# Maxima of q: rounded parts computed first and sent by a second DMA queue, unrounded maxima kept in PSUM

## The chip, the cores and the metric

One NeuronCore of a Trainium2 chip runs the whole program: TensorE (PE) multiplies matrices into PSUM, VectorE (DVE), ScalarE (ACT) and GpSimd (POOL) do the rest, and SyncE (SP) issues DMAs; ScalarE has a DMA queue too. The metric is the device time of one execution in microseconds (us), as the median of three runs.

## What is computed

Attention with a feature map, then two MLPs. For each of 4 batches and 8 heads, with 576 positions and 64 features a head:

```python
proj = x @ w_phi                                    # 64 -> 128, for q and for k
proj = proj - max(abs(proj), axis=-1)               # one maximum per position
phi  = concat(exp(proj), exp(-proj))
num  = phi_q @ (phi_k.T @ v);  den = phi_q @ sum(phi_k) + 1e-6
x    = num / den                                    # 2304 x 512 over all heads
x    = ((x @ w1) * (x @ w2)) @ w3 @ w_out           # first MLP, 1024 wide
h    = max(x @ w_in, 0);  out = (h * h) @ w_out2    # second MLP, 2048 wide
```

All inputs are fp32. Products that need the precision are made of three passes over a rounded "high" part and a "low" part, the rest that rounding leaves.

## The kernel before

Heads go two at a time: a *pair* is two heads of one batch, so there are 16 pairs, numbered 0 to 15 here. The attention part runs one *slot* a pair. The order inside a slot is written out by hand: `START` (line 29) is the prologue, `SLOT` (line 35) a list of step names; `step` (line 677) looks each name up and calls it for the pair that it is due for, and every engine then executes its own instructions in the order in which the steps issued them. In slot t, project_q, project_k, the peaks, exp and values work on pair t, the turning of q and k (turn_k, high_k, low_k, turn_q, high_q, low_q) on pair t+1, and the output, keep and the denominators on pair t-1. Even pairs also project the tail positions of k for two pairs (project_k2, peak_k2, less_k2, exp_k2); odd pairs instead turn tails for the next two (turn_tails, keep_tails, low_tail). Between these steps run decode steps of the MLP weights.

The maxima of q take this way. `project_q` (lines 369 to 382) leaves the projection in PSUM, three banks that one pair at a time can use. `max_q` (VectorE, line 387) reduces it to a 128 x 36 tile of maxima. `max_rows` (TensorE, line 395) transposes that. `max_parts` (lines 397 to 408) folds four groups of columns into the final 36 x 32 maxima `m`, makes a rounded copy `mh[:, 0]` by a second reduction, subtracts for the low part `mh[:, 1]`, and two DMAs write the two parts as rows 0 and 1 of `mrow` (SBUF to SBUF, 4.5 KB each). `minus_q` (line 414) multiplies `mrow` by a matrix of -1 and adds the result onto the projection in PSUM. `exp_q` (line 421) reads that twice for the two exponentials. The next pair's project_q writes the same PSUM banks, so it stands behind both.

The part of `SLOT` that matters: `peak_k0 max_rows high_k less_k0 max_parts w-1 late store_x exp_k0 out ... keep`. On ScalarE this is high_k, exp_k0 (two exponentials), keep (a copy), exp_k1, high_q, in odd slots keep_tails, and exp_q twice. On VectorE it is less_k0, the three instructions of max_parts, peak_k1, less_k1, low_k, denominators, low_q, decode work, and reciprocals, whose transpose is the last before the next max_q.

The PSUM banks with tag "o" (two of them) serve pm, po and pd in turn.

Of the kernel before, what the change touches and what calls it, by code (L numbers as in the profile page):

```python
# [9 lines left out]
F32 = mybir.dt.float32  # L10
# [3 lines left out]
ALU = mybir.AluOpType  # L14
AX = mybir.AxisListType
PSUM = bass.MemoryType.PSUM

P = 128
# [26 lines left out]
def attention_then_mlps(ctx: ExitStack, tc: tile.TileContext, q, k, v, w_phi, w1, w2, w3, wo, wi2, wo2, out):  # L45
    nc = tc.nc
# [28 lines left out]
    ident = const.tile([P, P], F32, name="ident")  # L75
# [128 lines left out]
    with ExitStack() as actx:  # L204
        att = actx.enter_context(tc.tile_pool(name="att", bufs=2, side="right"))
        ps = actx.enter_context(tc.tile_pool(name="ps", bufs=3, space=PSUM))

        def bank(name, tag="t", bufs=3):
            return ps.tile([P, 512], F32, tag=tag, bufs=bufs, name=name)
# [48 lines left out]
        nb = S // 32  # L258
# [132 lines left out]

        def max_rows(z):

            z["pm"] = bank(f"pm_{z['nm']}", "o", 2)[:, 0:P]
            nc.tensor.transpose(z["pm"], z["m1"], ident)

        def max_parts(z):
            pm = z["pm"][0:2 * nb]
            m = att.tile([2 * nb, 32], F32, tag="m", name=f"m_{z['nm']}")
            nc.vector.tensor_reduce(m, pm.rearrange("p (a r) -> p r a", a=4), AX.X, ALU.max)  # L400
            mh = att.tile([2 * nb, 2, 32], F32R, tag="mh", name=f"mh_{z['nm']}")
            nc.vector.tensor_reduce(mh[:, 0], pm.rearrange("p (a r) -> p r a", a=4), AX.X, ALU.max)
            nc.vector.tensor_tensor(out=mh[:, 1], in0=m, in1=mh[:, 0].bitcast(F32), op=ALU.subtract)
            z["mrow"] = mrow
            for s in range(2):
                nc.sync.dma_start(
                    z["mrow"][s:s + 1].bitcast(F32).rearrange("s (k r) -> s k r", r=32), mh[:, s].bitcast(F32)
                )

# [136 lines left out]
        w2h, w3s_at, queue, loaded, halves = {}, {}, [], [], []  # L546
# [55 lines left out]
        def even(f, *at):  # L602
# [3 lines left out]
        steps = {  # L606
            "keep_values": (-1, keep_values),
            "project_q": (0, project_q), "max_q": (0, max_q), "max_rows": (0, max_rows), "max_parts": (0, max_parts),
            "minus_q": (0, minus_q), "exp_q0": (0, lambda z: exp_q(z, 0)), "exp_q1": (0, lambda z: exp_q(z, 1)),
            "turn_k": (1, turn_k), "high_k": (1, high_k), "low_k": (1, low_k),  # L610
# [82 lines left out]
        with tc.manual_schedule(engines=mine):  # L693
            for entry in START:
                name, t = entry.split("/")
# [16 lines left out]
    def lunit(dtype, shape, name, tag="w", bufs=RIGHT):  # L712
        return late.tile([P] + shape, dtype, tag=tag, bufs=bufs, name=name)
# [207 lines left out]
    with tc.manual_schedule(engines=mine):  # L921
# [95 lines left out]
        for at, (b, n) in enumerate(mlp2):  # L1017
            cs, nt = nxt, n // P
            ops = None
            for j in range(NR):  # L1020
# [25 lines left out]
                r = lunit(F32R, [2, 512], f"r_{b}_{j}", "g", 3)  # L1046
# [50 lines left out]
```

## Time and profile before

| what | value |
|---|---|
| median of 3 runs | 939.31 us (939.11 to 940.91) |
| the profiled execution | 940.55 us, of which its span 938.8 us |
| TensorE busy | 919.8 us, 98% of the span |
| TensorE weight loads busy | 758.8 us, 81% |
| VectorE busy | 545.3 us, 58% |
| ScalarE busy | 382.6 us, 41% |
| GpSimd busy | 249.2 us, 27% |
| attention part | 0 to about 192 us |

The shares of busy time are means over very different stages: attention takes the first fifth, the rest is nearly all matrix multiplication. A wait is read from the time lines and from the view of waits, where "A <- B" says that A was released by B. A row of several instructions is one group: its start, the stretch that it covers, and how many there are.

### The profile page before, as it was taken

How to read it: one execution, taken by the hardware profiler on the slowest of the kernel's cores; microseconds unless marked ns; L12 is line 12 of the kernel's file. 1: busy time of each engine (PE TensorE's matmuls, PEld its weight loads, DVE VectorE, ACT ScalarE, POOL GpSimd, SP SyncE). 2: the span in 40 equal slices, each digit the busy share in tenths (PEclk: the TensorE clock that was granted, in tenths of full speed). 3: DMA queues.
4: the chain of work that ended last, by engine and by line, in shares of the span. 5: the costliest groups of instructions: out<-in, count | busy, mean ns of one | idle time of the engine just before them, and what ended most of it. 6: DMA issues, size and time to landing. Idle time of an engine off the chain costs nothing.

```text
span 938.8 us, 14821 instructions
## 1 busy us (share of the span) xinstructions
PE 919.8 (98%) x5897; PEld 758.8 (81%) x5897; DVE 545.3 (58%) x892; ACT 382.6 (41%) x689; POOL 249.2 (27%) x304
## 2 busy tenths in 40 slices
PE   8999999999999999999999999999999999999997
PEld 6777777778888988888988888888888888888896
DVE  6888888878656456666856688852224223322332
ACT  4777777643422433432333344342223223222322
POOL 2655566453121123333423145520000000000000
PEclk9999999999999999999999999999999999999999
DMA  6455556245242334254542433211002000200100
GB/s 178 124 154 152 139 157 198 78 144 172 73 135 66 114 114 156 68 202 157 173 176 93 142 118 107 90 46 44 1 1 90 1 0 1 68 1 1 39 8 22
DMA packets 81109, 89.22 MB, mean 95 GB/s; under 512 B 44624, under 2 KB 65680, under 8 KB 81040
## 3 DMA queue, kind: packets, MB, share of 16 engines
q1 hardware_dynamic: 79712, 87.72, 29.5%
q8 instruction: 46, 0.75, 0.3%
q10 hardware_dynamic: 1328, 0.56, 0.3%
q14 instruction: 23, 0.19, 0.1%
HBM read 69.76 MB, written 18.35 MB: 94 GB/s over the span
## 4 chain that ended last, share of the span: by engine, by line
PE 88%; DVE 6%; ACT 3%; DMA 2%; issue 1%; SPq 0%; ACTq 0%
PE ph L183 21%; PE op L905 21%; PE yp L887 11%; PE pb L183 11%; PE pa L183 10%; PE pf L844 5%; PE po L459 2%; PE pkv L432 2%; DMA mrow<-mh 2%; PE pk L250 1%; PE pq L380 1%; DVE kmax L348 1%; ACT qp L421 1%; DVE m L387 1%; PE pd L481 1%
## 5 line engine op out<-in xcount | busy, mean ns | idle before, releaser
L905 PE MATMUL op<-w_w,r 128*128 128x512 f32 x864 | 209.6, 390 | 0.1
L905 PEld LDWEIGHTS op<-w_w,r 128*128 128x128 f32 x864 | 161.1, 188 | 33.4 <-ACT r L1047 0.5
L183 PE MATMUL ph<-y,w_w 128*128 128x512 f32 (+1 forms) x768 | 163.9, 362 | 0.0
L1041 DVE SCALAR_TENSOR_TENSOR r<-ph,t 128x512 f32<-128x512 f32 (+1 forms) x80 | 51.1, 638 | 187.8 <-ACT t L1039 187.8
L183 PEld LDWEIGHTS ph<-y,w_w 128*128 128x128 f32 x768 | 133.3, 189 | 23.8
L1039 ACT ACTIVATE t<-ph 128x512 f32<-128x512 f32 (+1 forms) x80 | 44.5, 556 | 215.4 <-PE ph L183 215.4
L887 PE MATMUL yp<-g,w3o 128*128 128x512 f32 (+1 forms) x480 | 106.1, 370 | 0.0
L129 POOL TENSOR_TENSOR dt_w<-dt_w,dy_w 128x512 f32<-128x512 f32 x48 | 62.9, 1310 | 126.5 <-DVE dy_w L124 126.4
L887 PEld LDWEIGHTS yp<-g,w3o 128*128 128x128 f32 x480 | 83.7, 189 | 14.9 <-DVE yp L873 0.2
L183 PE MATMUL pa<-c,w_w12a 128*128 128x512 f32 (+1 forms) x432 | 93.6, 366 | 0.0
L183 PE MATMUL pb<-c,w_w12b 128*128 128x512 f32 (+1 forms) x432 | 93.6, 366 | 0.0
L183 PEld LDWEIGHTS pa<-c,w_w12a 128*128 128x128 f32 x432 | 75.1, 189 | 13.2
L183 PEld LDWEIGHTS pb<-c,w_w12b 128*128 128x128 f32 x432 | 75.2, 189 | 13.1
L1049 DVE TENSOR_TENSOR r<-r,r 128x512 fp32r<-128x512 f32 (+1 forms) x80 | 51.0, 638 | 41.2 <-ACT r L1047 37.5
L966 DVE TENSOR_TENSOR g<-pb,a 128x512 f32<-128x512 f32 (+1 forms) x39 | 24.8, 636 | 83.9 <-PE pb L183 79.4
L139 POOL TENSOR_TENSOR w_w<-dt_w,w_w 128x512 fp32r<-128x512 f32 x32 | 48.5, 1518 | 84.2 <-ACT w_w L137 84.2
L1047 ACT ACTIVATE r<-r 128x512 fp32r<-128x512 f32 (+1 forms) x80 | 47.2, 590 | 55.9 <-DVE r L1041 55.9
L506 POOL TENSOR_SCALAR rc<-dc 32x9 f32<-32x9 f32 x128 | 45.4, 355 | 57.6 <-DVE dc L496 50.5
L968 ACT ACTIVATE g<-g 128x512 fp32r<-128x512 f32 (+1 forms) x39 | 23.0, 589 | 91.6 <-DVE g L966 91.6
L958 ACT COPY a<-pa 128x512 f32<-128x512 f32 (+1 forms) x39 | 21.2, 543 | 81.0 <-PE pa L183 81.0
L365 ACT ACTIVATE kp<-kp 128x512 f32<-128x512 f32 (+1 forms) x80 | 46.9, 588 | 17.6 <-DVE kp L358 15.5
L121 DVE TENSOR_SCALAR dy_w<-dt_w 128x512 int32<-128x512 int32 x48 | 49.8, 1038 | 0.7
(135 smaller groups left out, 1277.6 us busy)
## 6 DMA issues: line engine op xcount, KB each, us to landing
x<-x_hbm SPq DMA_DIRECT2D x16, 512.0 KB
raw_w<-in_moe_w_dram SPq DMA_DIRECT2D x16, 512.0 KB
raw_w<-in_moe_w_in_dram SPq DMA_DIRECT2D x16, 512.0 KB
raw_w<-in_moe_w_out_dram SPq DMA_DIRECT2D x16, 512.0 KB
qm<-in_q_dram SPq DMA_DIRECT2D x32, 128.0 KB
km<-in_k_dram SPq DMA_DIRECT2D x16, 256.0 KB
vs<-in_v_dram SPq DMA_DIRECT2D x32, 128.0 KB
raw_wo<-in_moe_w_out_dram SPq DMA_DIRECT2D x8, 512.0 KB
```

Of the source, the lines that this page charges most:

```text
L121: nc.vector.tensor_scalar(out=e, in0=t, scalar1=-(1 << 23), scalar2=None, op0=ALU.bitwise_and)
L129: nc.gpsimd.tensor_tensor(out=w, in0=t.bitcast(F32), in1=e.bitcast(F32), op=ALU.add)
L139: nc.gpsimd.tensor_tensor(out=dst[:, 1], in0=w[0], in1=dst[:, 0].bitcast(F32), op=ALU.subtract)
L183: nc.tensor.matmul(ps[:, 0:n], a, c, start=kk + i == 0, stop=kk == KD - 1 and i == 2)
L365: nc.scalar.activation(z["kp", j][:, :, s, :], z["kp", j][:, :, 1, :], AF.Exp, scale=1.0 - 2.0 * s)
L506: nc.gpsimd.tensor_scalar(out=z["rc2"][i * 32:(i + 1) * 32, s, :], in0=z["dc"][at * 32:(at + 1) * 32, :], scalar1=1e-6, scalar2=None, op0= ...
L844: nc.tensor.matmul(pf, a, c, start=g + j + n == 0, stop=g == 1 and j == 3 and n == 2)
L887: nc.tensor.matmul(blk.yp[i][:, 0:blk.n], a, d, start=c % HG + s == 0, stop=c % HG == HG - 1 and s == 2)
L905: nc.tensor.matmul(ops[i], a, d, start=j + s == 0, stop=j == NR - 1 and s == 2)
L1041: nc.vector.scalar_tensor_tensor(out=r32[:, 0:n], in0=ph[:, 0:n], scalar=0.0, in1=t[:, 0:n], op0=ALU.max, op1=ALU.mult)
L1047: nc.scalar.activation(r[:, 0, 0:n], r32[:, 0:n], AF.Copy)
L1049: nc.vector.tensor_tensor(out=r[:, 1, 0:n], in0=r32[:, 0:n], in1=r[:, 0, 0:n].bitcast(F32), op=ALU.subtract)
```

## The change

`max_parts` makes the rounded maxima with its first reduction and the unrounded ones with its second. The unrounded ones no longer have an SBUF tile: they go to columns 128 to 159 of the PSUM bank that holds the transposed maxima, so `z["pm"]` is now the whole bank. The high part's DMA is issued by ScalarE, the low part's by SyncE. `START` and `SLOT` stay as they are.

```diff
         def max_rows(z):
 
-            z["pm"] = bank(f"pm_{z['nm']}", "o", 2)[:, 0:P]
-            nc.tensor.transpose(z["pm"], z["m1"], ident)
+            z["pm"] = bank(f"pm_{z['nm']}", "o", 2)
+            nc.tensor.transpose(z["pm"][:, 0:P], z["m1"], ident)
 
         def max_parts(z):
-            pm = z["pm"][0:2 * nb]
-            m = att.tile([2 * nb, 32], F32, tag="m", name=f"m_{z['nm']}")
-            nc.vector.tensor_reduce(m, pm.rearrange("p (a r) -> p r a", a=4), AX.X, ALU.max)
+            view = z["pm"][0:2 * nb, 0:P].rearrange("p (a r) -> p r a", a=4)
             mh = att.tile([2 * nb, 2, 32], F32R, tag="mh", name=f"mh_{z['nm']}")
-            nc.vector.tensor_reduce(mh[:, 0], pm.rearrange("p (a r) -> p r a", a=4), AX.X, ALU.max)
+            nc.vector.tensor_reduce(mh[:, 0], view, AX.X, ALU.max)
+            m = z["pm"][0:2 * nb, P:P + 32]
+            nc.vector.tensor_reduce(m, view, AX.X, ALU.max)
             nc.vector.tensor_tensor(out=mh[:, 1], in0=m, in1=mh[:, 0].bitcast(F32), op=ALU.subtract)
             z["mrow"] = mrow
-            for s in range(2):
-                nc.sync.dma_start(
+            for s, queue in enumerate((nc.scalar, nc.sync)):
+                queue.dma_start(
                     z["mrow"][s:s + 1].bitcast(F32).rearrange("s (k r) -> s k r", r=32), mh[:, s].bitcast(F32)
                 )
```

On ScalarE, in the slot of pair 9 (kT and qT are the turned k and q, kp the exponents of k, nd the kept numerators, tT the tails, qp the exponentials of q), before:

```order
L291 ACTIVATE kT_2_1819<-pkt_2_1810 128x512
L365 ACTIVATE kp_1_0_1821<-kp_1_0_1821 128x4x128 x2
L488 COPY nd_0_1861<-po_0_1835 128x512
L365 ACTIVATE kp_1_1_1859<-kp_1_1_1859 128x4x128 x2
L291 ACTIVATE qT_2_1885<-pqt_2_1863 128x512
L291 ACTIVATE tT_2_1890<-ptt_2_1869 128x256
L421 ACTIVATE qp_1_1892<-pq_1_1776 128x1152 x2
```

and the same place now:

```order
L291 ACTIVATE kT_2_1810<-pkt_2_1801 128x512
L406 DMA mrow<-mh_1_1814 1x36x32
L365 ACTIVATE kp_1_0_1812<-kp_1_0_1812 128x4x128 x2
L488 COPY nd_0_1851<-po_0_1825 128x512
L365 ACTIVATE kp_1_1_1849<-kp_1_1_1849 128x4x128 x2
L291 ACTIVATE qT_2_1875<-pqt_2_1853 128x512
L291 ACTIVATE tT_2_1880<-ptt_2_1859 128x256
L421 ACTIVATE qp_1_1882<-pq_1_1767 128x1152 x2
```

The DMA of the high part now stands between high_k and exp_k0 of every slot; nothing else moved on ScalarE.

On VectorE, in the same slot (pm is the transposed maxima, kmax the peaks of k), before:

```order
L358 TENSOR_TENSOR kp_1_0_1821<-pk_1_0_1790,kmax_1_0_1815 128x4x128
L400 TENSOR_REDUCE m_1_1823<-pm_1_1817 36x32
L402 TENSOR_REDUCE mh_1_1825<-pm_1_1817 36x32
L403 TENSOR_TENSOR mh_1_1825<-m_1_1823,mh_1_1825 36x32
L348 TENSOR_REDUCE kmax_1_1_1857<-pk_1_1_1798 128x4
```

and now:

```order
L358 TENSOR_TENSOR kp_1_0_1812<-pk_1_0_1781,kmax_1_0_1806 128x4x128
L400 TENSOR_REDUCE mh_1_1814<-pm_1_1808 36x32
L402 TENSOR_REDUCE pm_1_1808<-pm_1_1808 36x32
L403 TENSOR_TENSOR mh_1_1814<-pm_1_1808,mh_1_1814 36x32
L348 TENSOR_REDUCE kmax_1_1_1847<-pk_1_1_1789 128x4
```

The two reductions changed places, and the unrounded result is written to PSUM and read from there; the count and the neighbours are the same.

On SyncE, around the same slot's maxima (qm, km and vs are loads of q, k and v, raw_w12a of a weight), before:

```order
L236 DMA qm_3_1771<-in_q_dram 128x4x64 x2
L227 DMA km_3_1774<-in_k_dram 128x2x256
L406 DMA mrow<-mh_1_1825 1x36x32 x2
L105 DMA raw_w12a_1830<-in_moe_w_dram 128x4x128
L533 DMA x_hbm_1_81<-xm_1_1582 128x1024
```

and now:

```order
L236 DMA qm_3_1762<-in_q_dram 128x4x64 x2
L227 DMA km_3_1765<-in_k_dram 128x2x256
L406 DMA mrow<-mh_1_1814 1x36x32
L105 DMA raw_w12a_1820<-in_moe_w_dram 128x4x128
L533 DMA x_hbm_1_81<-xm_1_1574 128x1024
```

One of the two DMAs to mrow left SyncE; the loads before and behind it stand as they stood.

## Rows read from the trace of the kernel before

**Rows 1.** Windows: stretch, length, busy us of PE, PEld, DVE, ACT, POOL; clock, DMA, GB/s

```profile
60.00:120.00 60.00, 56.99 (x817) 44.44 (x815) 52.49 (x99) 47.64 (x85) 35.97 (x66) 1.00 0.53 143
...
400.00:600.00 200.00, 200.00 (x951) 168.37 (x950) 140.38 (x204) 74.19 (x133) 73.15 (x53) 1.00 0.41 141
```

**Rows 2.** Waits, 0 to 340 us: who <- for whom: us in total, times, longest

```profile
PE pq L414 <- DMA mrow<-mh: 6.4, 7, 1.2
...
ACT qp L421 <- PE pq L414: 2.2, 3, 1.0
```

**Rows 3.** DMA issues of two lines: count, ns min/median/max, first and last start

```profile
L406 SPq DMA_DIRECT2D mrow<-mh x32: 733/786/908, 13.1 to 183.5; - x32
...
L242 ACTq DMA_DIRECT2D ktl<-in_k_dram x2: 615/626/637, 2.7 to 3.7; - x2
```

**Rows 4.** Time line, start: start us, us, engine, line, what, count [idle before <-releaser]

```profile
2.74 1.59 ACTq L242 DMA_DIRECT2D ktl<-in_k_dram  x2
...
3.02 1.31 SPq L236 DMA_DIRECT2D qm<-in_q_dram  x2
...
4.36 1.28 ACT L148 ACT_TABLE_LOAD   x1 [4.36 <-DMA qm<-in_q_dram]
```

**Rows 5.** Time line of the slot of pair 9, with its end

```profile
114.75 0.27 DVE L400 TENSOR_REDUCE m<-pm 36x32 f32<-36x128 f32 x1
114.87 1.29 ACT L365 ACTIVATE kp<-kp 128x512 f32<-128x512 f32 x2
...
116.19 0.59 ACT L488 COPY nd<-po 128x512 f32<-128x512 f32 x1
...
116.80 1.30 ACT L365 ACTIVATE kp<-kp 128x512 f32<-128x512 f32 x2
...
118.14 0.60 ACT L291 ACTIVATE qT<-pqt 128x512 fp32r<-128x512 f32 x1
...
118.63 0.38 ACT L291 ACTIVATE tT<-ptt 128x256 fp32r<-128x256 f32 x1
118.77 0.69 DVE L294 TENSOR_TENSOR qT<-pqt,qT 128x512 fp32r<-128x512 f32 x1 [0.70 <-ACT qT L291]
...
119.01 2.15 ACT L421 ACTIVATE qp<-pq 128x1152 f32<-128x1152 f32 x2
...
121.36 0.96 PE L380 MATMUL pq<-qT,wss 64*128 64x512 f32 x6
...
122.96 1.34 DVE L387 TRANSPOSE_TENSOR_REDUCE m<-pq 128x36 f32<-128x1152 f32 x1
```

**Rows 6.** Time line of the slot of pair 8, with its end

```profile
103.39 1.29 ACT L365 ACTIVATE kp<-kp 128x512 f32<-128x512 f32 x2 [0.32 <-DVE kp L358]
...
105.32 1.29 ACT L365 ACTIVATE kp<-kp 128x512 f32<-128x512 f32 x2 [0.17 <-DVE kp L358]
...
106.52 0.58 ACT L291 ACTIVATE qT<-pqt 128x512 fp32r<-128x512 f32 x1
...
107.69 0.87 ACT L365 ACTIVATE kp<-kp 128x256 f32<-128x256 f32 x2 [0.58 <-DVE kp L358]
107.71 0.76 PE L414 MATMUL pq<-mrow,minus 128*128 128x512 f32 x3 [0.98 <-DMA mrow<-mh]
...
108.50 2.15 ACT L421 ACTIVATE qp<-pq 128x1152 f32<-128x1152 f32 x2
...
110.86 0.97 PE L380 MATMUL pq<-qT,wss 64*128 64x512 f32 x6
...
112.15 1.38 DVE L387 TRANSPOSE_TENSOR_REDUCE m<-pq 128x36 f32<-128x1152 f32 x1 [0.66 <-PE pq L380]
```

**Rows 7.** Time line: end of pair 0's slot, loads in pair 10's, pair 15's split of x

```profile
19.33 0.97 PE L380 MATMUL pq<-qT,wss 64*128 64x512 f32 x6 [0.71 <-ACT qp L421]
...
125.71 1.27 SPq L242 DMA_DIRECT2D ktl<-in_k_dram  x2
...
184.08 1.90 DVE L149 TENSOR_TENSOR x<-x,x 128x512 fp32r<-128x512 f32 x3 [1.27 <-ACT x L148]
```

## The prediction

> **What bounds the kernel now.** I read the busy time by stretch first. In the attention part (0 to 190 us) no engine is full: between 60 and 120 us TensorE is busy 56.99 of 60 us, VectorE 52.49, ScalarE 47.64, and they hand work to each other; later (400 to 600 us) TensorE alone is full, 200.00 of 200.00 [rows 1]. The change touches attention only, so it is worth what it does to the length of the sixteen slots there; a microsecond lost there is a microsecond lost at the end.
>
> Then the waits. TensorE waits 6.4 us in 7 places for the transfer that writes the rows of maxima, and ScalarE three times, 2.2 us, for the matmuls behind it [rows 2]. That is what the change could take away. Last I read two slots in order of time, pair 9 (odd) and pair 8 (even), to see which engine sets their ends.
>
> Odd pair 9 [rows 5]: on ScalarE exp_k0 starts at 114.87; keep, exp_k1, high_q, keep_tails and exp_q follow at 116.19, 116.80, 118.14, 118.63 and 119.01 almost without a gap, and exp_q ends at 119.01 + 2.15 = 121.16. The next project_q starts at 121.36. VectorE's low_q waited 0.70 us for ScalarE's high_q (118.77), and max_q of the next pair (122.96) shows no idle time before it: VectorE ran from low_q into it. So in an odd slot ScalarE's row of activations sets both the next project_q and, through low_q, the next max_q.
>
> Even pair 8 [rows 6]: ScalarE waits 0.17 before exp_k1 and 0.58 before exp_k2, TensorE waits 0.98 for the transfer (107.71), exp_q ends at 108.50 + 2.15 = 110.65 and the next project_q starts at 110.86. Here ScalarE has room.
>
> **The change, part by part.**
>
> *High part on ScalarE's queue.* In the order given above, the transfer stands between high_k and exp_k0 on ScalarE and waits for VectorE's first reduction. Queued behind the wait are exp_k0, keep, exp_k1, high_q and both exp_q: everything the slot needs from ScalarE. The reduction starts at 114.75 [rows 5]; I give it the 0.27 us of its kind, which is how far the trace's two reductions of this shape go, and 0.03 us of hand-over, so the transfer can be issued at 115.05. Its issue takes 0.786 us on SyncE (733 to 908 ns); ScalarE's own issues of loads take 0.626 us [rows 3]. Does the issue hold ScalarE's next instruction? The trace has one place: ScalarE's last two load issues run from 2.74 to 4.33, and its table load starts at 4.36 [rows 4] (the view names a transfer as what released it; the time fits the end of the issue). I take it as held. I take 0.79 for the issue, the row of the same transfer, and keep 0.62 and 0.91 as ends. Then 115.05 + 0.79 + 0.03 = 115.87 for exp_k0 against 114.87: **1.00 us later** in every slot, of which 0.18 is the wait for VectorE.
>
> What of that reaches the end of a slot? I take ScalarE's own pace from starts where nothing is waited for: keep to exp_k1 0.61 and high_q to keep_tails 0.49 [rows 5], exp_k1 to high_q 1.20 and exp_k2 to exp_q 0.81 [rows 6], and exp_k0 to keep the same 1.20, since both are a pair of exponentials of one shape.
> Odd: 115.87, keep 117.07, exp_k1 117.68, high_q 118.88 (was 118.14, **+0.74**), keep_tails 119.37, exp_q 119.75 (0.38 on, as before), end 121.90, project_q 121.95 (+0.59; I take 0.05 for this hand-over, an estimate between the 0.03 above and the 0.20 that lay there). VectorE's low_q moves by the same 0.74 and with it, having no gap, the next max_q. The later of the two counts: 0.74 per odd slot.
> Even: exp_k0 104.39, exp_k1 1.81 on at 106.20, high_q 107.40, exp_k2 107.89 (its input was there at 107.69), exp_q 108.70, end 110.85, project_q 110.90 against 110.86: **+0.04**. The waits of 0.17 and 0.58 and the slack before project_q swallow the rest. low_q moves by about half a microsecond; the 0.66 idle before the next max_q (112.15) covers it [rows 6].
>
> *Low part alone on SyncE.* It no longer stands behind the high part's issue, so it goes up to 0.79 us earlier [rows 3]. In the odd slots TensorE is not waiting for it. In the even slots TensorE's wait of about 1 us shrinks, but project_q then waits for exp_q, which the paragraph above puts at 110.85; at best, with ScalarE undisturbed, 110.86 could become 110.70, 0.16 us. I count this gain at 0, because ScalarE comes last now. Pairs 3 and 13 are odd slots in which ScalarE itself waited about 1.0 us for the transfer (two of the three waits in [rows 2]); there the 0.74 fits inside that wait, and I count 0.
>
> *Maxima in PSUM, rounded ones first.* Still two reductions and one subtraction. The subtraction now reads PSUM; bounded by itself as it stands and by one more reduction of 0.27 us, at most a tenth of a microsecond by my choice, and none of it counts: VectorE idles 0.70 before low_q in odd slots and waits for TensorE before max_q in even ones [rows 5, 6]. If that cover were gone it would cost 0.1 x 16 = 1.6 us. In even slots TensorE's wait for ScalarE's copy of the sums moves from turn_k to the second project_k; that copy is issued right behind exp_q, well before; nothing.
>
> *The first and the last slot.* Pair 0's slot ends on ScalarE: project_q waited 0.71 us for exp_q [rows 7]. In pair 15's slot ScalarE's split of x follows exp_k0, and VectorE waits 1.27 us for it [rows 7], then comes to the last peaks. I count the full 1.0 us for each.
>
> **Sum.** Odd pairs 1, 5, 7, 9, 11: 5 x 0.74 = 3.7. Pairs 0 and 15: 2.0. Seven even pairs: 7 x 0.04 = 0.3. Together **+6.0 us**. The profiled execution took 940.55 us (span 938.8 and 1.75 around it), so it would be 946.55; the median of the runs is 1.24 lower, 939.31, so I forecast **945.3 us**. With the issue at 0.62 every delay is 0.83: 5 x 0.57 + 2 x 0.83 = 4.5. With 0.91 it is 1.12: 5 x 0.86 + 2 x 1.12 + 7 x 0.16 = 7.7. About 1 us each way for waits on a late transfer that fall elsewhere gives the case's own range, 942.8 to 948.0.
>
> **Rivals.**
>
> *ScalarE is not held, and the transfer's head start counts (faster or equal).* If issuing ran beside the activations, five even slots would gain up to 0.16 and pairs 3 and 13 up to 0.7 each: 0.8 + 1.4 = 2.2, so 937.1 to 939.3, say 938.2. It decides where exp_k0 starts no more than 0.26 us later (an odd slot's own gaps: 1.32 - 1.20 before keep, 1.34 - 1.20 before high_q); 0.18 of that goes to the wait for VectorE, so the hold would have to be under 0.1 us. For: the trace shows no activation directly behind an issue. Against: the table load at 4.36 [rows 4]. Chance 0.12.
>
> *The two queues stand in each other's way (slower still).* In pairs 2, 6 and 10 SyncE is issuing four loads of tails when ScalarE's turn comes: in pair 10 the reduction would end near 122.96 + 2.60 + 0.27 = 125.83 (max_q to reduction as 112.15 to 114.75) and two issues run from 125.71 for 1.27 us [rows 5 to 7]. If one had to end first, ScalarE would wait 0.5 us, if both, 1.15; these slots have no room left, so 3 x 0.5 = 1.5 to 3.5 us: 946.8 to 948.8. Against: at the start two issues on SyncE take 1.31 us beside ScalarE's issues [rows 4], 0.65 each, as ScalarE's 0.626 [rows 3]; none is doubled. The Trainium skill's Perfetto Trace Analysis (DMA Instruction, HWDGE) says the descriptor generator is locked for exclusive use while one instruction is set up, and that the profiled row includes the wait for the lock; by that rule the 1.5 us above would be paid, and the rows at the start do not show a lock over a whole issue. Chance 0.13.
>
> *Only the ends of the part pay.* If odd slots have room that I read as none (0.20 us lies between exp_q's end and project_q, and decode work between low_q and max_q could give way), pairs 0 and 15 alone cost 2.0: 941.3, from 940.3 to 942.8. Against: no idle time is shown before max_q at 122.96. Chance 0.12.
>
> **How the numbers follow.** Forecast 0.63, rivals 0.12, 0.13 and 0.12. What this measurement can tell from no change is 0.2%, 1.9 us: 937.4 to 941.2. Faster takes the edge of the first rival, 0.02, and 0.05 out of the forecast's share for what I have not seen; within takes the first rival's other 0.10 and the lower third of the last, 0.04; slower the remainder. That is 0.07, 0.14 and 0.79. The range that leaves out about 2 in 10 is 940.4 to 948.2.
>
> **What would show it.** In the profile after: ScalarE's transfer issue about 0.8 us long, in front of exp_k0, and exp_k0 starting about 1.1 us after the first reduction's start instead of 0.12; TensorE's wait for the transfer shrunk from 6.4 us; its wait for exp_q grown from the few there are to most slots; idle time before low_q grown in odd slots; odd slots longer by 0.7, even ones unchanged. A start of exp_k0 at its old distance from the reduction, or a slot length unchanged in pairs 5, 7, 9 and 11, would make the forecast wrong.

## The result, and the profile after

The changed kernel takes 944.88 us (median of 6 runs, 944.62 to 945.66) against 939.25 us for the kernel before on the same chip (939.11 to 940.91): ratio 1.0058, 95% interval 1.0045 to 1.0071, so it is slower, by 0.6%. The forecast was 945.3 us. The profiled execution after took 944.62 us with a span of 942.8, 4.0 more than the span of before; the medians lie 5.6 apart, because the profiled execution of before was 1.3 above its median and that of after 0.3 below.

The issues of the two transfers, after (view of one line, the columns of [rows 3]):

```profile
L406 ACTq DMA_DIRECT2D mrow<-mh x16: 732/732/1357, 13.0 to 185.4; - x16
L406 SPq DMA_DIRECT2D mrow<-mh x16: 788/802/912, 13.4 to 185.9; - x16
```

ScalarE's issue takes 0.732 us, a little less than the 0.786 of the same transfer on SyncE [rows 3]; one of the sixteen, the first, takes 1.357. The waits, 0 to 340 us, after (columns of [rows 2]):

```profile
ACT kp L365 <- DVE mh L403: 14.9, 10, 3.9
DVE qT L294 <- ACT qT L291: 12.8, 15, 1.7
...
PE pq L380 <- ACT qp L421: 9.3, 12, 1.6
...
PE pq L414 <- DMA mrow<-mh: 2.6, 3, 1.3
```

and two of the same rows before:

```profile
DVE qT L294 <- ACT qT L291: 6.9, 9, 1.3
...
PE pq L380 <- ACT qp L421: 3.3, 4, 0.9
```

What the change was to remove went: TensorE's wait for the transfer fell from 6.4 to 2.6 us [rows 2]. What stands in its place is ScalarE: exp_k0 is shown waiting for the instructions of max_parts (the view names the subtraction; the transfer's issue lies between), VectorE waits for high_q in 15 slots instead of 9, and TensorE waits 9.3 us for exp_q before project_q instead of 3.3. The slot of pair 9, after, in order of time:

```profile
116.86 0.60 ACT L291 ACTIVATE kT<-pkt 128x512 fp32r<-128x512 f32 x1 [0.55 <-PE pkt L288]
117.40 0.27 DVE L400 TENSOR_REDUCE mh<-pm 36x32 fp32r<-36x128 f32 x1
117.71 0.73 ACTq L406 DMA_DIRECT2D mrow<-mh  x1
118.49 1.29 ACT L365 ACTIVATE kp<-kp 128x512 f32<-128x512 f32 x2 [1.03 <-DVE mh L403]
119.69 0.57 ACT L488 COPY nd<-po 128x512 f32<-128x512 f32 x1
120.15 1.30 ACT L365 ACTIVATE kp<-kp 128x512 f32<-128x512 f32 x2
121.35 0.58 ACT L291 ACTIVATE qT<-pqt 128x512 fp32r<-128x512 f32 x1
121.83 0.38 ACT L291 ACTIVATE tT<-ptt 128x256 fp32r<-128x256 f32 x1
121.97 0.69 DVE L294 TENSOR_TENSOR qT<-pqt,qT 128x512 fp32r<-128x512 f32 x1 [1.24 <-ACT qT L291]
122.09 2.15 ACT L421 ACTIVATE qp<-pq 128x1152 f32<-128x1152 f32 x2
124.30 0.96 PE L380 MATMUL pq<-qT,wss 64*128 64x512 f32 x6 [0.35 <-ACT qp L421]
126.15 1.34 DVE L387 TRANSPOSE_TENSOR_REDUCE m<-pq 128x36 f32<-128x1152 f32 x1
```

The reader is to see the gap that opens between 117.46, where high_k ends, and 118.49: first the reduction, then the issue, then exp_k0. Counted from the reduction's start, with the rows of before [rows 5]:

```
pair 9           before   after   later   predicted
exp_k0             0.12    1.09    0.97     1.00
keep               1.44    2.29    0.85     0.88
exp_k1             2.05    2.75    0.70     0.88
high_q             3.39    3.95    0.56     0.74
low_q (VectorE)    4.02    4.57    0.55     0.74
exp_q              4.26    4.69    0.43     0.74
next project_q     6.61    6.90    0.29     0.59
next max_q         8.21    8.75    0.54     0.74
```

The even slot of pair 8, after:

```profile
106.15 0.27 DVE L400 TENSOR_REDUCE mh<-pm 36x32 fp32r<-36x128 f32 x1
106.45 0.73 ACTq L406 DMA_DIRECT2D mrow<-mh  x1
106.87 0.80 SPq L406 DMA_DIRECT2D mrow<-mh  x1
107.23 1.29 ACT L365 ACTIVATE kp<-kp 128x512 f32<-128x512 f32 x2 [1.49 <-DVE mh L403]
...
109.37 0.68 PE L414 MATMUL pq<-mrow,minus 128*128 128x512 f32 x3
...
110.58 0.85 ACT L365 ACTIVATE kp<-kp 128x256 f32<-128x256 f32 x2
...
111.33 2.13 ACT L421 ACTIVATE qp<-pq 128x1152 f32<-128x1152 f32 x2
113.52 0.96 PE L380 MATMUL pq<-qT,wss 64*128 64x512 f32 x6 [1.01 <-ACT qp L421]
```

The reduction of the same slot before:

```profile
103.27 0.27 DVE L400 TENSOR_REDUCE m<-pm 36x32 f32<-36x128 f32 x1
```

The next project_q came 7.59 us after that (110.86 in [rows 6]); now it comes 7.37 us after the reduction (113.52). TensorE's minus_q (109.37) no longer waits for the transfer, as it did for 0.98 us in [rows 6], and no activation waits between exp_k0 and exp_q: the gaps of 0.17 and 0.58 in [rows 6] are used up. The ends of the part, after (end of pair 0's slot, then pair 15's):

```profile
14.37 1.29 ACT L365 ACTIVATE kp<-kp 128x512 f32<-128x512 f32 x2 [5.18 <-DVE kmax L348]
...
20.67 0.97 PE L380 MATMUL pq<-qT,wss 64*128 64x512 f32 x6 [1.63 <-ACT qp L421]
...
188.07 1.90 DVE L149 TENSOR_TENSOR x<-x,x 128x512 fp32r<-128x512 f32 x3 [2.23 <-ACT x L148]
```

Both waits of [rows 7] grew by about what exp_k0 was late: 0.71 to 1.63 and 1.27 to 2.23. By slot, from project_q to project_q, the profiled executions differ so:

```
prologue (first project_q 8.25 -> 8.70)            +0.45
pair 0                                             +0.89
pairs 1, 5, 7, 9, 11  .34 .33 .27 .28 .32          +1.54
pairs 3, 13           .20 -.69                     -0.49
pairs 2, 4, 6, 8, 10, 12, 14
                      .18 0 -.05 .05 -.06 .30 .21  +0.63
pair 15's project_q to the end                     +0.97
sum                                                +3.99   (spans 942.8 - 938.8 = 4.0)
```

The prologue's 0.45 lies ahead of the first maxima, where the change has no instruction; in the profiles of the experiments below the first project_q starts 0.16 us earlier to 0.87 later than before, so this row is taken as the scatter of single executions.

### The profile page after: what moved, and what is told of

It reads as the page before. It is cut to its first block, busy times and chain, and to the rows that moved or that the text cites. A ratio compares the mean times of both kernels' runs of the same rounds, so it can differ in the third digit from the quotient of the medians.

```text
span 942.8 us, 14823 instructions
## 1 busy us (share of the span) xinstructions
PE 920.6 (98%) x5897; PEld 758.8 (80%) x5897; DVE 545.4 (58%) x892; ACT 377.2 (40%) x689; POOL 242.8 (26%) x304
## 4 chain that ended last, share of the span: by engine, by line
PE 84%; DVE 5%; ACT 5%; DMA 3%; issue 1%; SPq 1%; ACTq 0%
PE ph L183 21%; PE op L905 21%; PE yp L887 11%; PE pb L183 10%; PE pa L183 10%; PE pf L844 5%; ACT kp L365 3%; DVE m L387 1%; ACT qp L421 1%; PE pkv L432 1%; PE pq L380 1%; DVE kmax L348 1%; DMA mrow<-mh 1%; PE po L459 1%; PE pw L177 1%
## 5 line engine op out<-in xcount | busy, mean ns | idle before, releaser
L506 POOL TENSOR_SCALAR rc<-dc 32x9 f32<-32x9 f32 x128 | 38.9, 304 | 54.1 <-DVE dc L496 47.1
```

## Experiments

Three things changed at once: who issues, the order of the reductions, and where the maxima stand. The theory: ScalarE is held in front of exp_k0, and that alone costs. The rivals: the new order or the PSUM operand costs; or each issue on ScalarE has a flat price, wherever it stands. Each result is the ratio to runs of the kernel before on the same chip, with its 95% interval.

**Both transfers on SyncE again.**

```diff
-            for s, queue in enumerate((nc.scalar, nc.sync)):
+            for s, queue in enumerate((nc.sync, nc.sync)):
```

> The changed kernel with both transfers of the maxima on SyncE's queue again; the rounded reduction first and the maxima in PSUM stay. Theory (ScalarE held by the issue): everything comes back, 938.9 us (938.0 to 939.6), exp_k0 starts 0.12 us after the first reduction's start as before, and no change from before in the typical slots, since the high part starts 0.2 us earlier and TensorE's end in even slots hangs on exp_k2 and exp_q. Rival (the new order of the reductions and the PSUM operand cost part of it): 941 us or more; all of it there: 944.9.

Measured 939.58 us against 939.80, ratio 0.9994 (0.9985 to 1.0003). The order and the PSUM operand cost nothing and bring nothing that this measurement can tell.

**The queue alone, on the kernel before.**

```diff
             nc.vector.tensor_reduce(m, pm.rearrange(...), AX.X, ALU.max)
             nc.vector.tensor_reduce(mh[:, 0], pm.rearrange(...), AX.X, ALU.max)
...
-            for s in range(2):
-                nc.sync.dma_start(
+            for s, queue in enumerate((nc.scalar, nc.sync)):
+                queue.dma_start(
```

> The kernel before with only the high part's transfer on ScalarE's queue: unrounded reduction first, maxima in SBUF. Theory: ScalarE's issue now waits for the second reduction, about 0.3 us later than in the changed kernel, exp_k0 at 1.4 us after the first reduction's start; the slots have no room left, so 947.5 us (946.0 to 949.5). Rival (the cost lies in PSUM and the reductions' order): 939 to 941. Rival (a flat price for each issue on ScalarE, 5.6/16 = 0.35 us): 944.9.

Measured 946.96 us, ratio 1.0070 (1.0054 to 1.0085): slower than the whole change. exp_k0 starts 1.28 us after the first reduction in nearly all slots. So putting the rounded reduction first (with the maxima in PSUM) does help, by 1.5 us (7.16 above before here, 5.63 there), but only because ScalarE now waits for it.

**The hold without the wait.**

```diff
             for s in range(2):
                 nc.sync.dma_start(...)
+            nc.scalar.dma_start(spare.bitcast(F32), minus[0:2 * nb, 0:32].bitcast(F32))
```

This is the end of max_parts in the kernel before; `(...)` stands for arguments that stay as they are, and `spare` is a new 36 x 32 tile that nothing reads.

> The kernel before, both transfers on SyncE, with one more transfer in each slot issued by ScalarE at the place where the changed kernel has its own; it copies 36 x 32 of a constant tile to an unused tile, so it waits for nothing. Theory: it starts when high_k ends (114.8 in pair 9's slot of before, 103.07 in pair 8's), so exp_k0 comes 0.70 us later in odd slots and 0.4 in even ones, against about 1.0 in the changed kernel; the odd slots swallow about 0.66, so only pairs 0 and 15 pay 0.7 each and the odd ones a little: 941.0 us (940.3 to 942.5). Rival (flat price for each issue, by whatever means): 944.9. Rival (an issue does not hold ScalarE): 939.3.

Measured 940.48 us against 939.80, ratio 1.0006 (0.9997 to 1.0016): nearly nothing, for sixteen issues of the same length. ScalarE in pair 9's slot of this kernel, with the first reduction on VectorE:

```profile
113.65 0.60 ACT L292 ACTIVATE kT<-pkt 128x512 fp32r<-128x512 f32 x1 [0.93 <-PE pkt L289]
113.71 0.73 ACTq L411 DMA_DIRECT2D spare<-minus  x1
114.20 0.27 DVE L401 TENSOR_REDUCE m<-pm 36x32 f32<-36x128 f32 x1
114.49 1.29 ACT L366 ACTIVATE kp<-kp 128x512 f32<-128x512 f32 x2 [0.24 <-DVE m L401]
```

The time came near the expectation, but the reason given for it was wrong. The issue does not begin when high_k ends, as was expected; it begins 0.06 us after high_k began and runs beside it. It holds only what is behind it: exp_k0 starts 0.05 after the issue's end, 0.29 after the reduction's start instead of 0.12. An issue that waits for nothing hides under the activation in front of it. In the changed kernel it cannot: it waits for the reduction, and by then high_k has ended (117.46 against 117.71 above). The wait itself is short; what it does is to take the cover away from the issue.

**Held twice.**

```diff
             for s, queue in enumerate((nc.scalar, nc.sync)):
                 queue.dma_start(...)
+            nc.scalar.dma_start(spare.bitcast(F32), minus[0:2 * nb, 0:32].bitcast(F32))
```

> The changed kernel with that same transfer of a constant issued by ScalarE right behind its transfer of the high part, so ScalarE is held twice. Theory (a hold, and slots whose room the first one used up): exp_k0 comes 0.75 us later again and nearly all of it reaches the end of all 16 slots: 12 us more, 956 us (953 to 958). Rival (a flat price of 0.35 for each issue): 950.5. Rival (the transfer on another queue, not the hold): 945.

Measured 958.82 us, ratio 1.0198 (1.0179 to 1.0216), a little above the range. In pair 8's slot:

```profile
112.07 0.74 ACTq L407 DMA_DIRECT2D mrow<-mh  x1
112.85 0.74 ACTq L411 DMA_DIRECT2D spare<-minus  x1
113.64 1.29 ACT L366 ACTIVATE kp<-kp 128x512 f32<-128x512 f32 x2 [2.28 <-DMA mrow<-mh]
```

Behind another issue the second one has no cover, and the first has used up the slots' room: 19.0 us above before instead of 5.6, so 13.4 more, 0.84 a slot, for 0.8 to 0.9 more of lateness. In the profile most slots are 0.8 to 0.9 longer than in the changed kernel, but those of pairs 13 and 15 are 1.6 longer: TensorE's granted clock fell to 0.50 there (last section). The flat price is refuted: it would have been 950.5 us.

**Queues exchanged: the low part on ScalarE.**

```diff
-            for s, queue in enumerate((nc.scalar, nc.sync)):
+            for s, queue in enumerate((nc.sync, nc.scalar)):
```

> The changed kernel with the two queues exchanged: the high part on SyncE, the low part on ScalarE, at the same place in front of exp_k0. Theory (what counts is how late exp_k0 starts): the low part is ready about 0.72 us after the first reduction's start, so exp_k0 starts at 1.50 instead of 1.08. The runs so far give 944.9 us at 1.08, 947.0 at 1.28 and 958.8 at 1.90; between the last two that is 951.1 us (949.0 to 952.5). Rival (the issue's own length counts, wherever it waits): 944.9, as the issues are as many and as long.

Measured 951.67 us, ratio 1.0131 (1.0117 to 1.0145). With exp_k0's typical start after the first reduction, the five kernels now read:

```
exp_k0 after reduction   0.12    1.08    1.28    1.55    1.9     us
time                     939.3   944.9   947.0   951.7   958.8   us
```

The same number of issues, of 0.73 to 0.77 us, costs 5.6 to 12.3 us by how late it lets exp_k0 start (the last column has twice as many issues). Not all of that is lateness itself. The profiled execution with the queues exchanged lost TensorE's clock three times; the first, in pair 5's slot (columns of [rows 1]):

```profile
66.50:70.60 4.10, 2.64 (x44) 2.18 (x39) 3.79 (x8) 3.02 (x7) 1.40 (x3) 1.00 0.45 99
70.70:74.00 3.30, 3.30 (x18) 2.97 (x18) 2.34 (x4) 1.39 (x3) 2.68 (x3) 0.50 0.43 120
```

TensorE was busy 2.64 of 4.10 us, waiting 1.46 of them for exp_q, and then ran with a granted clock of 0.50, which is 1.2 GHz. The slots of pairs 5 and 9 grew by 1.8 and 1.9 us, those of pairs 7 and 11, at 1.00, by 0.7 and 0.8. Of the four runs, the two with a mean clock of 0.993 took 952.2 and 952.9 us, the two with 0.998 took 951.0 and 951.1, so the order of the five kernels does not hang on it.

**Behind exp_k0 instead of in front.**

```diff
         def exp_k(z, j):
             ...
+            if j == 0:
+                send(z, 0, nc.scalar)
```

Here `send` issues the DMA of one part, 0 the high one and 1 the low one, and max_parts ends with `send(z, 1, nc.sync)`.

> The changed kernel with the high part's transfer still issued by ScalarE, but behind the two exponentials of exp_k0 instead of in front of them; the low part goes on SyncE where it went. Theory after the run with a transfer that waits for nothing (an issue runs beside the activation in flight, and holds only what is behind): exp_k0 starts 0.12 us after the first reduction again, the issue begins about 0.75 us after it, beside the second exponential, and ends near 1.5, so keep starts 1.5 to 1.6 after the reduction's start instead of 1.44 in the kernel before: nearly free, 939.5 us (938.3 to 940.5). Rival (each issue holds ScalarE for its whole 0.73 us behind whatever activation it follows): keep at 2.1 or later, 943.6 us (942.5 to 944.9).

Measured 941.04 us against 939.39, ratio 1.0018 (1.0008 to 1.0028): 0.5 us above the theory's range and 1.5 below the rival's. Pair 9's slot decides between them:

```profile
116.53 0.27 DVE L402 TENSOR_REDUCE mh<-pm 36x32 fp32r<-36x128 f32 x1
116.65 1.29 ACT L365 ACTIVATE kp<-kp 128x512 f32<-128x512 f32 x2
117.37 0.73 ACTq L411 DMA_DIRECT2D mrow<-mh  x1
118.14 0.59 ACT L493 COPY nd<-po 128x512 f32<-128x512 f32 x1 [0.20 <-PE po L464]
```

The issue runs beside the second exponential, and keep starts 1.61 after the reduction (116.53) instead of 1.44, as the theory has it. What still costs in this profile is at the ends (pair 0's issue took 1.59 us and its slot grew by 0.48, pair 15's by 0.45) and in two slots with a late transfer (pairs 8 and 14, 2.35 and 1.32; last section).

**Pairs 0 and 15 on SyncE.** In the changed kernel `nc.scalar if z["nm"] not in ("0_0", "3_3") else nc.sync` takes the place of `nc.scalar` ("0_0" is pair 0, "3_3" pair 15).

> The changed kernel with the high part of pairs 0 and 15 on SyncE, the other 14 on ScalarE. Theory: of the 5.6 us that the change costs, the two ends of the attention part are 1.9 (0.9 in pair 0's slot and 1.0 in pair 15's by the slots' lengths), so 943.0 us (942.3 to 943.8). Rival (only the ends pay): 939.5 to 940.5. Rival (the slots between pay all, the ends are hidden): 944.9.

Measured 943.91 us against 939.39, ratio 1.0044 (1.0031 to 1.0057), just above the range: 4.5 above before instead of 5.6, so 1.1 came back, not 1.9. Pair 1's slot shows why:

```profile
24.98 0.58 ACT L291 ACTIVATE kT<-pkt 128x512 fp32r<-128x512 f32 x1
25.25 1.35 ACTq L406 DMA_DIRECT2D mrow<-mh  x1
26.64 1.29 ACT L365 ACTIVATE kp<-kp 128x512 f32<-128x512 f32 x2 [1.08 <-DVE kmax L348]
```

The long issue is not pair 0's: it is the first one of its kind on ScalarE, and it moved to pair 1, whose slot grew by 0.93. Pair 0's slot gave back 0.7 us (0.89 to 0.16), and pair 1's took on 0.6 (0.34 to 0.93).

**Odd pairs alone, even pairs alone.** `nc.scalar if z["pr"] % 2 else nc.sync`, and its opposite.

> The changed kernel with ScalarE's transfer in the eight odd pairs alone; even pairs send both parts by SyncE. Theory (the price lies in the odd slots and pair 15): pair 15 pays 1.0, the first issue, now in pair 1, 0.6 beside pair 1's 0.3, the other odd slots 0.3 each: 939.4 + 3.3 = 942.7 us (941.8 to 943.6). Rival (the first prediction's term of 0.74 for an odd slot): 939.4 + 1.0 + 0.6 + 7 x 0.74 = 946.2. Rival (every pair pays alike): 942.1.

> The changed kernel with ScalarE's transfer in the eight even pairs alone; odd pairs send both parts by SyncE. Theory (an even slot covers the hold): pair 0 pays 0.9, the seven others 0.0 to 0.1 each: 939.4 + 1.2 = 940.6 us (939.8 to 941.5). Rival (every pair pays alike): 942.1. Rival (even slots only look free in the changed kernel because odd slots in front of them pay): 942.5 or more.

Measured 944.22 us (ratio 1.0050, 1.0038 to 1.0063) and 941.30 us (1.0013, 1.0005 to 1.0022) against 939.88. The second is within its range, the first 0.6 above. The two add up to the whole: 4.3 and 1.4 against 5.6. Of the odd pairs' 4.3, pair 15 is about 1.0 and the first issue about 0.6, by the profiles above; that leaves an estimate of 2.7 for seven odd slots, 0.39 each. The even slots cover the hold whether or not odd slots in front of them are late.

**Towards a better version.** The kernel that issues behind exp_k0, with an early issue in the prologue, and pair 15's high part on SyncE:

```diff
         def project_q(z):
+            if z["nm"] == "0_0":
+                nc.scalar.dma_start(spare.bitcast(F32), minus[0:2 * nb, 0:32].bitcast(F32))
...
-                send(z, 0, nc.scalar)
+                send(z, 0, nc.sync if z["nm"] == "3_3" else nc.scalar)
```

> The kernel whose high part is issued behind exp_k0's two exponentials, with two further edits: pair 15's high part goes by SyncE, and ScalarE issues one transfer of a constant in the prologue, behind keep_tails, where it idles for over 3 us. Theory: the first issue of a transfer between SBUF tiles on ScalarE takes 1.34 to 1.59 us, whichever pair it falls in, and the later ones 0.73; with the first one in the idle time, pair 0's takes about 0.73, which gives back 0.5 to 0.85 us, and pair 15 gives back 0.4: from 941.0 to 939.7 us (938.7 to 940.4). Rival (pair 0's issue is long because of the loads in flight at that time): pair 0's issue stays above 1.3 us, 940.6.

Measured 946.55 us, ratio 1.0072 (1.0055 to 1.0088): a clear miss. The first issue did what was expected (1.36 us in the idle prologue, pair 0's then 0.77). But pair 15's high part, sent from exp_k0's place, now stood behind other work on SyncE:

```profile
184.29 0.80 SPq L414 DMA_DIRECT2D mrow<-mh  x1
185.19 0.92 SPq L105 DMA_DIRECT2D raw_w<-in_moe_w_dram  x2
186.20 0.38 SPq L541 DMA_DIRECT2D x_hbm<-xm  x1
186.68 0.74 SPq L414 DMA_DIRECT2D mrow<-mh  x1
...
192.86 1.30 PE L422 MATMUL pq<-mrow,minus 128*128 128x512 f32 x3 [4.64 <-DMA mrow<-mh]
```

4.5 KB behind two loads of weights arrived some 6 us after its issue instead of 1.9, and TensorE waited 4.64 us. Behind the wait its granted clock was 0.50 (columns of [rows 1]), which is part of what this place cost:

```profile
191.45:198.20 6.75, 5.34 (x59) 4.49 (x61) 1.36 (x3) 3.19 (x5) 0.05 (x1) 0.50 0.27 108
```

With that one transfer at its old place:

```diff
         def exp_k(z, j):
             ...
-            if j == 0:
-                send(z, 0, nc.sync if z["nm"] == "3_3" else nc.scalar)
+            if j == 0 and z["nm"] != "3_3":
+                send(z, 0, nc.scalar)
...
-            send(z, 1, nc.sync)
+            for s in ((0, 1) if z["nm"] == "3_3" else (1,)):
+                send(z, s, nc.sync)
```

> As the kernel before it (high part behind exp_k0's exponentials on ScalarE, one early issue in the prologue), but pair 15's high part goes by SyncE at its old place, in front of the low part, and no longer behind the loads of weights. Theory (pair 15's 4.64 us wait came from the place of that one transfer): 946.55 less 4.6 and less what followed it, 941.0 us (939.0 to 941.7); if the slots between, each 0.1 to 0.25 us shorter than before, show in the median, 938.9. Rival (sending behind exp_k0 makes the transfers late in general): 943 us or more.

Measured 939.59 us against 939.99, ratio 1.0002 (0.9988 to 1.0016). The change's whole price is gone, and nothing is won: no version tried beats the kernel before by more than the measurement can tell. In the profile the slots of pairs 5 to 11 are together 1.1 us shorter than before (0.05 to 0.27 each), so there is a gain between the ends, but it does not show in the median. The runs spread from 937.9 to 944.0; the last section has what comes and goes there.

## Why the prediction came out as it did

The forecast was 945.3 us, the result 944.9. The mechanism was right, and the place; one term was twice its size, and another part of the working made up for it.

- **ScalarE is held before exp_k0: right.** 0.97 us later against 1.00 predicted; the issue took 0.73 instead of the 0.79 chosen from SyncE's row. What the prediction did not know is why the hold is paid whole: the experiment without a wait shows that an issue that waits for nothing lies beside the activation in front.
- **Odd slots, +0.74 each: the mis-sized term.** It measured 0.27 to 0.34 in the profile of five odd slots, and 0.39 by medians. Two steps failed. First, ScalarE's own pace: keep to exp_k1 takes 0.46 where nothing is waited for (119.69 to 120.15), not the 0.61 of [rows 5], and keep_tails to exp_q 0.26 (121.83 to 122.09), not 0.38. So those starts of before held small gaps which the view does not mark (exp_k1 started 0.02 after keep's end before, and starts 0.11 ahead of it now), and they took up part of the lateness: project_q moved 0.29, not 0.59. Second, "the later of the two counts": VectorE's max_q did move by 0.54, but even slots behind made good the difference. In the slots of pairs 6, 8 and 10 the next project_q comes 7.37 us after the first reduction (pair 8: 113.52 - 106.15) instead of 7.59 to 7.68 before, as minus_q no longer waits for the transfer; in pair 12's, where it had not waited (7.34 before), nothing was made good, and the slot grew by 0.30.
- **The low part's head start, counted at 0: wrong as a part.** It is those 0.2 to 0.3 us in three even slots (in pair 8's, part of it is a late transfer of before, last section), and there it went to making up for VectorE; in pair 13's slot it is 0.69 us.
- **Even slots, +0.3 in all:** 0.63 in the profile. Right in kind; the even pairs alone cost 1.4 us, of which pair 0 is 0.9.
- **Pairs 0 and 15, 1.0 each:** 0.89 and 0.97, right in size. But some 0.5 of pair 0's is the first issue's extra length, which the prediction did not know: its slot grew by 0.48 with a long issue behind exp_k0 and by 0.04 with the long one moved to the prologue.
- **Pairs 3 and 13, 0:** 0.20 and -0.69. Their transfers were late in the profile of before for a reason of their own (last section), and again in that of after. Pair 13's landed 2.9 us behind the later issue in both, and that issue begins 0.72 us after the first reduction instead of 1.41: the low part's head start, which shortened this slot by 0.69. Pair 3's landed 3.8 us behind it instead of 2.9, which ate the head start up.
- **PSUM and the order of the reductions, 0:** right, by the run with both transfers on SyncE.
- **The sum and the median.** The sum was 6.0 from the profiled execution; the profiled executions differ by 4.1. Taking 1.24 off for the median of before then assumed that after would be profiled as far above its median; it was 0.3 below. The two errors, 1.9 too much and 1.5 too little, nearly cancel. The right total owes something to luck; the right sign and place do not.

The rivals. "ScalarE is not held" is refuted: even the issue that waits for nothing held exp_k0 to its end, 0.29 us behind the reduction instead of 0.12. What is true of it is that such an issue lies beside the activation in front, so little of it is paid. "Only the ends pay" is refuted: with pairs 0 and 15 on SyncE 4.5 us remain. "The two queues stand in each other's way" is not seen. In pair 10's slot of the changed kernel, SyncE is issuing tails when ScalarE's turn comes:

```profile
127.92 1.27 SPq L242 DMA_DIRECT2D ktl<-in_k_dram  x2
...
129.01 0.73 ACTq L406 DMA_DIRECT2D mrow<-mh  x1
...
129.43 0.81 SPq L406 DMA_DIRECT2D mrow<-mh  x1
```

ScalarE's issue starts 0.18 us before SyncE's ends and takes 0.73; SyncE's own, beginning 0.42 into ScalarE's, takes 0.81. By the rule of the Trainium skill (Perfetto Trace Analysis, DMA Instruction, HWDGE) that one instruction at a time has the descriptor generator for itself, and that the profiled row includes the wait for it, one of these rows would be lengthened if that lasted for the whole issue; neither is, by more than a few hundredths. With the queues exchanged, where 15 of ScalarE's 16 issues began 0.4 us into one of SyncE, the median was 0.77 instead of 0.73 us, 0.04 more.

## What to carry to other kernels

On ScalarE the issue of a DMA cost next to nothing here while an activation ran in front of it, and held the engine for its whole length, 0.73 us, when it first had to wait for data and the engine had run dry; so put it behind work that lasts until the data are there, and not in front of the next link of the critical row. When a delay passes through a row of instructions, take the engine's pace from a place where it was really late, since small unmarked gaps swallow a part. A queue that carries big loads is no place to move a small transfer to without looking at what it then stands behind.

## What the runs showed of the hardware that was not expected

**The first issue.** ScalarE's first transfer between SBUF tiles took 1.34 to 1.59 us to issue in every kernel, in pair 0, in pair 1, or in the idle prologue; the later ones 0.72 to 0.81. ScalarE had issued loads before it, so it is not the first use of the queue. SyncE's first of the kind is longer too, 0.91 to 0.92 in every kernel against 0.73 to 0.82 later. Why, no run tells.

**Late transfers and instruction packets.** A pair's transfers usually have landed 1.9 to 2.3 us after the later of their issues began. In the thirteen profiles (207 slots, that of pair 15 above aside) they took longer in 48, all in pairs 2, 3, 8, 10, 13 and 14, and in each of these the DMA packets hold one of 8 or 16 KB on a queue of kind "instruction" beside the transfer. Such a packet also lies beside 26 transfers that were on time, 21 of them in the same pairs, so by itself it does not make one late. The stretch of pair 8's transfer in the kernel before, where TensorE waited 0.98 us [rows 6]; the columns are queue and kind: packets, MB, share of the 16 engines:

```profile
q1 hardware_dynamic: 314, 0.23, 19.1%
q8 instruction: 1, 0.02, 1.7%
```

That one packet took 1.08 us on its DMA engine, and the transfers' last semaphore updates came 1.4 us after its end. In the kernel before the late ones took 2.8 to 2.9 us, in the kernels that use both queues up to 4.8. In the same pairs a transfer is late in one profile and not in another, so this can be a part of what spreads the runs of one kernel. It was read, not tested: no kernel here moved the code, and that the packet is the cause is not shown.

**The clock behind a long wait.** Over the attention part TensorE's granted clock is 1.00 in the profiles of before and after. In five experiments it fell to 0.50 for a few microseconds, each time behind a stretch in which TensorE had waited: the hold without the wait (165.3 to 168.6, pair 13's slot, 2.65 us longer than before), held twice (170.4 to 173.7 and 194.3 to 197.5), the queues exchanged (three times), behind exp_k0 (108.6 to 111.9, pair 8's slot, 2.35 longer) and the kernel with pair 15 behind the loads (twice). In the first, the fourth and the last a late transfer stood in front of the fall. So a wait can cost more than its length, and this too spreads the runs: of the twelve runs of the last version, those at 941.4 to 944.0 us have mean clocks of 0.996 to 0.998, those at 939.4 to 939.8 us 1.000, though the three fastest, at 937.9 to 938.3, have 0.998 and 0.999. No run here separates the late transfers from the clock.
